# Turning q by the crossbar from chunk 2 on, in two halves, with the next chunk's loads planned behind the first half

## The chip, the cores and the metric

One core of a Trainium2 chip. The metric is device microseconds of one execution of the whole program on that core; medians of several runs are given. A program on one core has no second die to compare with, so a run counts as slow only if it lies over 1.5% above the fastest of its kernel; comparisons use the other runs.

Every ratio below is the mean time of one kernel's fast runs over that of the kernel before's fast runs of the same rounds on the same chip, so it is not quite the ratio of the quoted medians.

## The reference, cut to what matters

```python
kv  = einsum('bhsd,bhse->bhde', k, v)            # 8 batches, 8 heads, 576 rows, head size 64
out = einsum('bhsd,bhde->bhse', q, kv)
out = out / sqrt(mean(out*out, -1) + 1e-6) * g_norm
x   = out as [4608, 512]                          # rows of all batches, heads side by side
h   = x @ w_in                                    # [4608, 1024]
solu = h * softmax(h);  ln = layernorm(solu) * g_ln
return ln @ w_out                                 # [4608, 512], float32
```

## The kernel before

The rows are worked off in nine chunks of 512: chunk c below 8 is the first 512 rows of batch c, chunk 8 collects the last 64 rows of each batch. Per chunk TensorE makes k'v (`kv_mm`), o (`o_mm`, two halves of four heads), the sums of squares over heads (`s_mm`), eight projections (`h_mm`), the sums over d_ff and the eight halves of the output (`out_mm`). ScalarE does squares, logarithms and exponentials, VectorE (DVE) products and scaling, GpSimd (POOL) squares and sums in SBUF, and it also issues all loads that cast to bf16.

`o_mm` needs q with the head's columns on the partitions, so q has to be turned. Up to chunk 3 TensorE turns it (eight 128x128 transposes for each half of the heads, into the one PSUM bank `misc`, once into `h`, and a copy out); from chunk 4 on the DMA crossbar turns all of it from SBUF to SBUF, issued from the SP queue.

All instructions are ordered by a small list scheduler in the kernel (the planner). Each piece has an engine, an assumed length and a list of pieces that must be over first; pieces are put out in the order of their planned times. A piece that is listed as needed is an order in the plan. It is a semaphore wait on the chip only if the later instruction reads or overwrites what the earlier one wrote or read.

```python
class Plan:                                        # cut
    def order(self):
        ...
            if n[0] == "qT" and engine == "sp":    # a crossbar turn
                if queue > t + 1.0:                # loads still queued by the plan's reckoning
                    length, queue = 2.2 * length, queue + 2.0
            free[engine] = t + length
            done[n] = t + length + {"pe": 0.2, "sp": 2.5}.get(engine, 0.12)
            if load:
                queue = max(queue, t + length + 1.0) + load
                done[n] = queue + 1.3
...
    XBAR = tuple(range(4, NC))                     # chunks whose q the crossbar turns
...
    for b in range(B):                             # loads of k, v, q, issued from POOL
        behind = [] if b < 2 else [("h_mm", 0, 0)] if b == 2 else [("h_mm", b - 3, 2 if b == 3 else 0)]
        ...
    def q_turn(c):
        t = T["qT", c] = tile_of(("qT", c), [128, H, 2, 128], BF16)
        nc.sync.dma_start_transpose(
            t.rearrange("q h y p -> q (h y) p"), T["q", c].rearrange("p h j d -> p (h j d)")
        )
```

The softmax here doesn't subtract the row's maximum and nothing guards it: scores larger than these inputs give would overflow.

## Time and profile before

| | kernel before |
|---|---|
| median | 201.49 us (201.22 to 203.51, 4 runs) |
| span of the profiled run | 200.0 us, mean granted TensorE clock 0.996 |
| TensorE busy | 183.5 us (92%) |
| ScalarE / DVE / POOL busy | 141.1 / 125.0 / 128.7 us |
| first projection of chunk 1 | 48.01 us |
| first o of chunk 2 | 47.66 us |
| loads of chunks 3, 4, 5 leave POOL (k) | 30.70, 36.90, 64.02 us |

TensorE's share of the whole span says little; the prediction below shows the lines stretch by stretch.

### The profile page before, as it was taken

The page shows a single profiled execution, that of the slowest core. Times are in us where ns is not written, and L with a number is a line of the kernel's source. Part 1 is how long each engine was busy: PE and PEld are TensorE (multiplying, and loading weights), DVE is VectorE, ACT ScalarE, POOL GpSimd, SP SyncE. Part 2 cuts the span into 40 slices and gives each one's busy share as a digit, 9 for nine tenths or more (in the row PEclk, how much of TensorE's full clock was granted, in tenths as well). Part 3 has the DMA queues.
Part 4 walks back from the last instruction along what each step waited for, and adds up shares of the span by engine and source line. Part 5 has one row for each costly group of instructions (what it writes and reads, how often), then busy time and mean ns, then how long its engine had stood idle before and what let it go on. Part 6 is the DMA issues. An engine that isn't in the chain of part 4 may idle for free.

```text
span 200.0 us, 4091 instructions
## 1 busy us (share of the span) xinstructions
PE 183.5 (92%) x1614; PEld 83.3 (42%) x1614; DVE 125.0 (62%) x236; ACT 141.1 (71%) x244; POOL 128.7 (64%) x137
## 2 busy tenths in 40 slices
PE   7988986879699989999999899999999999999990
PEld 2342444345354435444444343544445454444430
DVE  3346669358785759768566856867594757665350
ACT  2028867986998799878889496979779386556421
POOL 7953679700699996957797487387484828846200
PEclk9999999999999999999999999999999999999998
DMA  4999999999994999999999982226021111211206
GB/s 51 178 198 286 326 200 201 202 203 239 248 200 67 151 200 167 196 196 223 186 166 197 179 210 69 107 71 157 17 91 52 52 56 52 108 52 52 107 11 198
DMA packets 39986, 29.62 MB, mean 148 GB/s; under 512 B 11800, under 2 KB 34336, under 8 KB 39968
## 3 DMA queue, kind: packets, MB, share of 16 engines
q0 software_dynamic: 24208, 17.30, 56.9%
q1 hardware_dynamic: 15472, 11.54, 19.8%
q10 hardware_dynamic: 288, 0.52, 0.9%
q8 instruction: 12, 0.20, 0.4%
q14 instruction: 6, 0.05, 0.1%
HBM read 32.51 MB, written 9.44 MB: 210 GB/s over the span
## 4 chain that ended last, share of the span: by engine, by line
PE 59%; DMA 20%; ACT 8%; POOL 6%; DVE 3%; issue 2%; POOLq 0%
PE out_ps L577 24%; PE h_ps L456 22%; DMA q_sb<-in_q_dram 11%; DMA w_out_f<-in_moe_w_out_dram 9%; PE misc_ps L520 4%; PE o_ps L337 3%; PE s_ps L358 3%; ACT rst_sb L366 2%; ACT e_sb L464 2%; PE o_ps L577 2%; ACT lss_sb L362 2%; POOL q_sb L230 1%; POOL v_sb L223 1%; DVE x_sb L379 1%; POOL k_sb L223 1%
## 5 line engine op out<-in xcount | busy, mean ns | idle before, releaser
L456 PE MATMUL h_ps<-x_sb,w_in_sb 128*128 128x512 bf16 x276 | 70.3, 379 | 2.2 <-DVE x_sb L379 1.2
L577 PE MATMUL out_ps<-w_out_sb,u_sb 128*128 128x512 bf16 x272 | 68.8, 379 | 0.8 <-DVE ob_sb L587 0.6
L482 POOL TENSOR_TENSOR usq_sb<-u_sb 128x512 bf16<-128x512 bf16 x51 | 52.7, 1042 | 22.0 <-DVE u_sb L471 21.7
L488 POOL TENSOR_TENSOR es_sb<-e_sb 128x512 bf16<-128x512 f32 x36 | 45.7, 1271 | 28.6 <-ACT e_sb L464 28.4
L471 DVE TENSOR_TENSOR u_sb<-h_ps,e_sb 128x512 bf16<-128x512 f32 x69 | 47.1, 687 | 25.6 <-ACT e_sb L464 25.1
L464 ACT ACTIVATE e_sb<-h_ps,zero_t 128x512 f32<-128x512 f32 x69 | 47.2, 685 | 15.5 <-PE h_ps L456 12.9
L456 PEld LDWEIGHTS <-w_in_sb 128*128 128x128 bf16 x288 | 27.1, 98 | 35.9 <-issue 5.7
L577 PEld LDWEIGHTS <-u_sb 128*128 128x128 bf16 x288 | 27.0, 98 | 34.0 <-issue 3.8
L587 DVE TENSOR_SCALAR ob_sb<-out_ps,rstd 128x512 f32<-128x512 f32 x33 | 24.4, 745 | 10.4 <-ACT rstd L556 5.4
L379 DVE SCALAR_TENSOR_TENSOR x_sb<-o_ps,g_rep,rst_sb 128x512 bf16<-128x512 f32 x32 | 23.9, 748 | 7.0 <-ACT rst_sb L366 6.7
L352 ACT ACTIVATE osq_sb<-o_ps,zero_t 128x512 bf16<-128x512 f32 x31 | 19.9, 683 | 9.4 <-PE o_ps L337 9.4
L366 ACT ACTIVATE rst_sb<-lss_sb,zero_t 128x512 f32<-128x512 f32 x32 | 23.3, 728 | 0.6
L362 ACT ACTIVATE lss_sb<-s_ps,eps_t 128x512 f32<-128x512 f32 x32 | 22.0, 688 | 0.6 <-PE s_ps L358 0.3
L480 ACT ACTIVATE usq_sb<-u_sb,zero_t 128x512 bf16<-128x512 bf16 x21 | 15.1, 720 | 4.9 <-DVE u_sb L471 4.9
L300 ACT CAST kvd<-misc_ps 64x128 bf16<-64x128 f32 (+1 forms) x24 | 7.5, 313 | 11.8 <-DVE kvd L298 11.3
L358 PE MATMUL s_ps<-osq_sb,head_mean 128*128 128x512 bf16 x34 | 12.9, 381 | 0.7 <-ACT lss_sb L362 0.4
L198 PE MATMUL s_ps<-zeros 128*128 128x512 bf16 x28 | 10.3, 498 | 1.4 <-DVE zeros L159 1.2
L230 POOL DMA_DIRECT2D q_sb<-in_q_dram x10 | 8.5, 854 | 4.2 <-DMA k_sb<-in_k_dram 1.6
L223 POOL DMA_DIRECT2D k_sb<-in_k_dram x10 | 7.8, 782 | 3.4 <-DMA w_in_sb<-in_moe_w_in_dram 1.8
L298 DVE CAST kvd<-misc_ps 64x256 bf16<-64x256 f32 (+1 forms) x16 | 6.1, 380 | 5.1 <-ACT kvd L300 3.1
L529 DVE STREAM_TRANSPOSE sumT_sb<-misc_ps 128x512 f32<-128x512 f32 x8 | 5.7, 711 | 5.7 <-PE misc_ps L520 5.7
L285 PEld LDWEIGHTS <-k_sb 96*64 96x64 bf16 x384 | 7.0, 112 | 4.1 <-issue 4.0
(81 smaller groups left out, 133.7 us busy)
## 6 DMA issues: line engine op xcount, KB each, us to landing
out_dram<-ob_sb SPq DMA_DIRECT2D x34, 256.0 KB, 2.5
k_sb<-in_k_dram POOLq DMA_DIRECT2D x6, 576.0 KB, 12.0
v_sb<-in_v_dram POOLq DMA_DIRECT2D x6, 576.0 KB, 12.1
q_sb<-in_q_dram POOLq DMA_DIRECT2D x6, 512.0 KB, 14.1
w_out_f<-in_moe_w_out_dram POOLq DMA_DIRECT2D x1, 2048.0 KB, 18.5
k_sb<-in_k_dram POOLq DMA_DIRECT2D x4, 288.0 KB, 12.6
v_sb<-in_v_dram POOLq DMA_DIRECT2D x4, 288.0 KB, 12.9
q_sb<-in_q_dram POOLq DMA_DIRECT2D x4, 256.0 KB, 13.1
```

The costliest lines, as they stand in the source:

```text
L352: nc.scalar.activation(out=t[:, :], in_=T[("o", *i)].rearrange("p a b c -> p (a b c)"), func=AF.Square, bias=zero_t[:, :])
L358: nc.tensor.matmul(t[:, :], head_mean[:, :], T["osq", i][:, :], start=True, stop=True)
L362: nc.scalar.activation(out=t[:, :], in_=T["s", i][:, :], func=AF.Ln, bias=eps_t[:, :])
L366: nc.scalar.activation(out=t.rearrange("p a b c -> p (a b c)"), in_=T["lss", i][:, :], func=AF.Exp, scale=-0.5, bias=zero_t[:, :])
L379: nc.vector.scalar_tensor_tensor(out=T["x", c][:, 2 * hf:2 * hf + 2, z], in0=T["o", c, hf, z][:, :, :, :], scalar=g_rep[:, :], in1=T["rst" ...
L456: nc.tensor.matmul(t[:, :], w_in_sb[:, dt, f * 128:(f + 1) * 128], T["x", c][:, dt].rearrange("p a b c -> p (a b c)"), start=(dt == 0), st ...
L464: nc.scalar.activation(out=T["e", c, f // 2][:, f % 2, :], in_=T["h", c, f][:, :], func=AF.Exp, bias=zero_t[:, :])
L471: nc.vector.tensor_tensor(out=T["u", c][:, f, :], in0=T["h", c, f][:, :], in1=T["e", c, f // 2][:, f % 2, :], op=MUL)
L482: nc.gpsimd.tensor_tensor(out=dst, in0=src, in1=src, op=MUL)
L488: nc.gpsimd.tensor_tensor(out=T["es", c][:, n, :], in0=e[:, 0, :], in1=e[:, 1, :], op=ADD)
L577: nc.tensor.matmul(T["acc", c, m][:, :], T["u", c][:, f, m * 128:(m + 1) * 128], w_out_sb[:, f, :], start=(f == 0), stop=(f == NF - 1),)
L587: nc.vector.tensor_scalar_mul(out=t[:, :], in0=T["acc", c, m][:, :], scalar1=T["rstd", c][:, m:m + 1])
```

## The change

Its intent: take the last turns off TensorE and the copies off DVE (chunks 2 and 3), let o of the first four heads start when half of the turn has landed, and keep the next chunk's loads out of the turn's way by planning them behind its first half.

```diff
-                    length, queue = 2.2 * length, queue + 2.0
+                    length, queue = 2.2 * length, queue + length
...
-    XBAR = tuple(range(4, NC))
+    XBAR = tuple(range(2, NC))
...
-        behind = ... [("h_mm", b - 3, 2 if b == 3 else 0)]
+        behind = ... [("qT", b - 1, 0)] + ([("h_mm", b - 3, 0)] if b > 3 else [])
...
-    def q_turn(c):
-        t = T["qT", c] = tile_of(("qT", c), [128, H, 2, 128], BF16)
+    def q_turn(c, hf):
+        if hf == 0:
+            T["qT", c] = tile_of(("qT", c), [128, H, 2, 128], BF16)
+        hs = slice(4 * hf, 4 * hf + 4)
         nc.sync.dma_start_transpose(
-            t.rearrange(...), T["q", c].rearrange("p h j d -> p (h j d)")
+            T["qT", c][:, hs].rearrange(...), T["q", c][:, hs].rearrange("p h j d -> p (h j d)")
         )
...
-            plan.add(("qT", c), "sp", 4.0, ...)
+            for hf in range(2):
+                plan.add(("qT", c, hf), "sp", 2.0, ...)
...
-                     [("qT", c) if c in XBAR else ("qT", c, hf), *kvs],      # what o_mm needs
+                     [("qT", c, hf), *kvs],
```

## The prediction

> **What bounds the kernel now.** I read the table of busy time by stretch first, because a share over the whole span mixes stages. Columns: stretch and its length; then for each engine busy us and instructions; last the granted clock, the DMA share and GB/s.
>
> ```profile
> core 0: us, PE busy (x) PEld busy (x) DVE busy (x) ACT busy (x) POOL busy (x), PEclk, DMA share, GB/s
> ...
> 40.00:48.00 8.00, 6.85 (x106) 3.91 (x106) 5.71 (x14) 5.58 (x11) 0.41 (x1) 1.00 1.32 220
> 48.00:56.00 8.00, 6.37 (x88) 3.27 (x85) 5.90 (x11) 7.29 (x13) 3.90 (x4) 1.00 1.28 237
> 56.00:64.00 8.00, 7.97 (x50) 3.68 (x48) 5.23 (x9) 7.38 (x13) 8.00 (x8) 1.00 0.82 118
> 64.00:72.00 8.00, 7.47 (x99) 3.52 (x97) 4.75 (x8) 6.33 (x13) 7.98 (x10) 1.00 1.14 167
> 72.00:80.00 8.00, 7.42 (x93) 3.60 (x90) 6.89 (x15) 7.87 (x17) 6.39 (x7) 1.00 1.10 181
> 112.00:120.00 8.00, 7.00 (x40) 2.96 (x38) 5.71 (x10) 5.71 (x10) 5.37 (x6) 1.00 0.84 193
> ```
>
> The reader is to see two regimes. From about 55 us on TensorE is close to full, and in every 8 us stretch from 80 to 192 us except the one at 112 it shows 8.00 of 8. There the end moves only with TensorE work taken away or with its few gaps (0.03 + 0.53 + 0.58 us between 56 and 80, 1.0 at 112). Before 56 us it has gaps: 1.15 and 1.63 us in the two stretches at 40 and 48, and 1.79 and 1.23 in those at 24 and 32 (not printed here). So the turns of q are worth their full TensorE time only where TensorE is full; earlier they lie partly in gaps.
>
> Then the timeline about the turns of chunks 2 and 3 that the change removes (start, duration, engine, line, operation, output <- inputs, count; in brackets the idle time before it and its releaser):
>
> ```profile
> 44.95 0.61 PE L308 MATMUL misc_ps<-ident,q_sb 128*128 128x128 bf16 x8
> ...
> 47.12 0.61 PE L308 MATMUL misc_ps<-ident,q_sb 128*128 128x128 bf16 x8
> ...
> 47.66 0.41 PE L337 MATMUL o_ps<-qT_sb,kvd 64*64 64x256 bf16 x8
> ...
> 48.12 1.26 ACT L352 ACTIVATE osq_sb<-o_ps,zero_t 128x512 bf16<-128x512 f32 x2 [1.53 <-PE o_ps L337]
> ...
> 54.02 1.27 ACT L464 ACTIVATE e_sb<-h_ps,zero_t 128x512 f32<-128x512 f32 x2
> ...
> 54.72 0.62 PE L308 MATMUL misc_ps<-ident,q_sb 128*128 128x128 bf16 x8 [1.63 <-DMA q_sb<-in_q_dram]
> ...
> 55.62 1.04 PE L456 MATMUL h_ps<-x_sb,w_in_sb 128*128 128x512 bf16 x4
> ```
>
> At 54.72 TensorE waited 1.63 us for chunk 3's q. That is not all the turn's fault: the next projection (55.62) needs an h bank, and those two banks are freed only after the two exponentials of 54.02 to 55.29 on ScalarE. ScalarE is busy 7.29 and 7.38 us of 8 here, so it is the pace-setter, and it had lost 1.53 us just before, waiting for chunk 2's o (48.12).
>
> Third, the turns and loads that exist already:
>
> ```profile
> L322 SPq DMA_TRANSPOSE qT_sb<-q_sb x4: 1631/1928/2036, 62.8 to 114.0; - x4
> ...
> DMA to landing us min/median/max: 4.3/4.4/6.8
> ```
>
> The minimum of 4.3 and the maximum of 6.8 us are a whole q (16 blocks of 128x128) on an otherwise quiet DMA and beside loads: the slow one, issued at 62.79, met chunk 5's loads from 64.02 on.
>
> **What the Trainium skill says.** "VectorE: DVE Perf Modes", section "The three transpose paths", gives 390 ns for a 128x128 bf16 turn on TensorE and 1309 ns by the crossbar. The trace has much less for both in a stream: eight turns in 0.61 us, sixteen crossbar blocks in 4.3 to 4.4 us. The measured ones decide, but the order is the same: the crossbar is slower and only pays because it frees engines. "Advanced Engine Details and Errata", section "X-Bar Transpose (TRN2)", expects 350-400 GB/s; 0.52 MB in 4.4 us is 119 GB/s with start-up, and while turns ran alone the DMA table showed some 210 to 220, so the trace does not agree. "DMA: Bandwidth & Descriptors", section "Issuing engines are not separate DMA queues", says that DMAs of all issuers share the 16 engines and interleave: the 6.8 against 4.3 us agrees. That is why the change plans loads behind the turn.
>
> **The change part by part.**
>
> Removed. Chunks 2 and 3 each lose two TensorE turns (8 matmuls, 0.61 us as shown, 0.45 us in the chain where pipelining overlaps them with the next work) and two DVE copies of 0.68 us (693 ns at most in the tile view). TensorE: 4 x 0.45 = 1.8 us, at most 4 x 0.61 = 2.4. DVE: 4 x 0.68 = 2.7 us, off the path, as DVE is busy 5.2 to 5.9 of 8 there. Of the TensorE time, the two turns of chunk 2 (44.95 and 47.12) lie where it waits anyway for x of chunk 1 (the first projection of chunk 1 starts at 48.01): worth 0. The turn at 54.72 is half hidden by ScalarE. The turn at 57.57 is in a full stretch: worth 0.45. Together 0.45 to 0.9.
>
> Added. Two more whole turns in halves, four crossbar issues, about 1 us of the SP queue each (estimate: half of 1.93), which is free there. A turn alone takes some 3.1 us of all DMA engines (the hardware queue's 31.2% share of the 10 us from 60 to 70). Cutting a turn in two should let the first half land about 1 us before the whole one would (estimate from the 1.9 us issue), so o of heads 0 to 3 can start earlier.
>
> Moved. The loads of chunk 3 are ordered after the first half-turn of chunk 2, no longer after the third projection of chunk 0. This is order on the POOL queue only, not a semaphore: POOL was idle from 40.4 to 50.8 us, so I expect them to go out as soon as chunk 0's last sums leave POOL, at about 34.5 instead of 30.70. Chunk 2's q then has the DMA more to itself and lands before 43.2 us (28.75 + 14.4 at present); I estimate 36 to 41. Add 4.4 to 6.8: its turn lands at 41 to 47.5, against a present DVE copy that ends at 46.5. So o of chunk 2 can start about 1 us earlier and fill part of the 1.53 us ScalarE gap: worth 1.1 us in a stretch that ScalarE paces. Chunk 4's loads move most: now at 36.90, they come behind chunk 3's first half-turn, at about 60 to 64. They must share POOL with the squares and sums of chunk 1, where POOL shows 8.00 of 8 busy; three issues of 0.8 to 0.9 cost 2.5 us of it.
>
> Sum: 0.7 (turns) + 1.1 (ScalarE starts chunk 2 earlier) + 0.4 (part of the gap at 48 to 56 that was the wait for q) - 0.6 (POOL and late loads, next part, weighted) = 1.6 us. 201.25 - 1.6 = 199.6 us.
>
> **The rivals.**
>
> *Late loads turn into TensorE waits.* The loads now form a cycle: load, turn, next load. From k's issue to q's landing takes 14.1 us (64.02 to 65.60 + 12.5), plus 4.4 for the turn: 18.5 us, while a chunk takes about 17.3 us of TensorE (sums at 104.48, 121.60, 138.78). If the plan thinks loads land sooner than they do, TensorE reaches the k-v product or o of chunks 4 and 5 before the data. At present those are at 68.0 and 77.8 for chunk 4; with loads at 60 to 64, v lands at 71 to 75 and the turn at 78 to 82. The planner knows of the delay and can put other projections first, and o of chunk 4 is needed only for h of chunk 4, far later. Against it too: the slack is regained later, as o of chunk 6 starts at 114.7 and its turn would land at about 111. Should it happen, 1 to 4 us are lost: 200.5 to 203.5.
>
> *POOL becomes the bound.* The one gap of TensorE after 80 us (1.0 at 113.66) came from such a thing: exponentials waited 2.25 us for POOL, which had been issuing loads at 99.8 to 102.8. One more chunk's issues in a busy stretch could make another gap of 1 us; moving the others could also remove this one. I put it at plus or minus 1.
>
> *The turns were hidden anyway.* Then only the 0.45 us remains and the time is 200.8.
>
> *More is freed than I count.* With no turns in the single misc bank of PSUM, and DMA relieved of chunk 4's loads until 55 us, all the gaps from 40 to 56 (2.8 us) could go, with the turns' 1.8: 196.7. Against it: ScalarE has 7.3 of 8 us of work there, which the change does not lessen.
>
> **Range and chances.** The best case gives 196.7, the bad one 203.5, the middle 199.6. I take 196.8 to 203.2 for 8 in 10. Faster by over 2% means under 197.2, which needs nearly every gap gone: 0.13. Slower by over 2% means over 205.3, worse than my stalls add up to: 0.08. Within 2%: 0.79.
>
> **What would show each step right or wrong.** No turns on TensorE after 40 us: 32 matmuls and 4 DVE copies fewer. The loads of chunk 3 near 34.5 us and of chunk 4 at 60 to 64. ScalarE's gap of 1.53 us before chunk 2's squares gone or under 0.5, and TensorE over 7 of 8 us in the stretch from 48 to 56. First half-turns that land in 3.5 to 6 us. The prediction is wrong if waits for k, v or turned q appear on TensorE at 66 to 96 us with more than 2 us in total, if the first projection of chunk 1 moves from 48 us by more than 2, or if the total falls below 197 because the gaps before 56 us had another cause than ScalarE.

## The result, and the profile after

The changed kernel takes 210.73 us (209.86 to 211.59, 4 runs) against 201.49: ratio 1.0436, interval 1.0355 to 1.0517. It is slower by over 2%, outside the range of the prediction. All its runs are of the fast state; the profiled one has a span of 208.8 us and a mean clock of 0.964.

The same table of stretches for the changed kernel, with the same columns:

```profile
40.00:48.00 8.00, 6.54 (x60) 2.98 (x54) 5.98 (x10) 5.99 (x12) 0.00 (x0) 1.00 1.28 230
48.00:56.00 8.00, 1.52 (x11) 0.58 (x11) 0.74 (x2) 0.96 (x3) 3.25 (x3) 0.65 1.33 177
56.00:64.00 8.00, 7.95 (x33) 2.99 (x33) 4.01 (x6) 5.51 (x10) 4.77 (x5) 0.71 0.40 78
64.00:72.00 8.00, 5.56 (x66) 2.59 (x66) 3.54 (x6) 5.69 (x10) 5.38 (x6) 0.93 0.01 2
72.00:80.00 8.00, 7.95 (x59) 2.95 (x59) 4.97 (x11) 6.70 (x13) 5.95 (x7) 0.86 1.01 142
```

From 48 to 56 us TensorE works 1.52 us where it had worked 6.37, ScalarE 0.96 instead of 7.29. The clock is granted at 0.65 to 0.93 in the stretches from 48 to 80 us; before, it was 1.00 in all of them. From 72 us on TensorE is nearly full again. From 48 to 72 us it works 15.0 us instead of 21.8, in part at the lower clock, so most of the loss is made there. Later marks agree, though pieces come in another order now: the sums over d_ff of chunk 2 (the squares' part) started at 83.89 us before and at 94.21 now, the last ones at 189.36 and 198.29, 8.9 us later.

The timeline of the changed kernel around it (POOL's issues of chunk 3's loads, the two half-turns of chunk 2, ScalarE, TensorE):

```profile
33.49 0.82 POOL L223 DMA_DIRECT2D k_sb<-in_k_dram  x1
34.30 0.77 POOL L223 DMA_DIRECT2D v_sb<-in_v_dram  x1
35.06 0.90 POOL L230 DMA_DIRECT2D q_sb<-in_q_dram  x1
...
42.48 6.88 SPq L324 DMA_TRANSPOSE qT_sb<-q_sb  x2
...
45.94 1.46 PE L459 MATMUL h_ps<-x_sb,w_in_sb 128*128 128x512 bf16 x6 [0.21 <-DVE x_sb L381]
...
54.48 0.64 PE L339 MATMUL o_ps<-qT_sb,kvd 64*64 64x256 bf16 x8 [7.08 <-DMA qT_sb<-q_sb]
...
55.16 1.27 ACT L354 ACTIVATE osq_sb<-o_ps,zero_t 128x512 bf16<-128x512 f32 x2 [7.04 <-PE o_ps L339]
```

The loads that were "planned behind the first half" of the turn left POOL at 33.49 us, nine microseconds ahead of that turn. Nothing on the chip made them wait for the turn: POOL issued them as soon as chunk 0's last sums were done (three sums from 29.82, 3.71 us) and had no other work before them. The turn was issued at 42.48, when chunk 2's q had just landed (27.85 + 14.2 = 42.05). TensorE then did two projections of chunk 1 and stood 7.08 us before the first o of chunk 2, and ScalarE stood as long.

How long the first half was under way until it landed, that is until its data had arrived, from the list of DMA issues, in a window that starts at its issue (count, then us from issue to landing):

```profile
qT_sb<-q_sb SPq DMA_TRANSPOSE x1, 12.0
```

And the DMA queues from 40 to 45 us (packets, MB, share). Queue q0 carries POOL's loads, q1 the stores and turns from SP:

```profile
q0 software_dynamic: 1387, 1.02, 132.4%
q1 hardware_dynamic: 1, 0.00, 0.1%
```

In these 5 us the loads moved 1387 packets. Queue q1 moved one, although a store had been issued at 41.45 and the turn at 42.48. The half-turn landed at 54.5 us, together with the last of chunk 3's loads (q: 35.06 + 19.6 = 54.7).

The lower clock fits the Trainium skill in kind: "TensorE: Matmul & The Clock Gate", section "Part 1: The HAM clock gate", says that the array falls to half clock after an idle window of about 3.4 us and comes back after a busy one. The lengths here are others: TensorE idled from 47.40 us, the clock was 1.00 until 50.2 and 0.50 from 50.4 on; work resumed at 54.48, and the clock was still 0.50 from 60.0 to 60.5. It fell once more at 70.8 us, after a wait of only 2.39 us.

### The profile page after: what moved, and what is told of

Same layout as the page of the kernel before. It is cut to its first block, busy times and chain, and to the rows that moved or that the text cites. A ratio compares the mean times of both kernels' runs of the same rounds, so it can differ in the third digit from the quotient of the medians.

```text
span 208.8 us, 4013 instructions
## 1 busy us (share of the span) xinstructions
PE 184.0 (88%) x1557; PEld 81.9 (39%) x1582; DVE 123.0 (59%) x232; ACT 142.3 (68%) x244; POOL 129.0 (62%) x137
## 4 chain that ended last, share of the span: by engine, by line
PE 63%; DMA 20%; DVE 4%; ACT 4%; POOL 4%; issue 2%; POOLq 0%; SPq 0%; ACTq 0%
PE h_ps L459 24%; PE out_ps L580 23%; DMA w_out_f<-in_moe_w_out_dram 8%; DMA qT_sb<-q_sb 7%; DMA v_sb<-in_v_dram 5%; PE misc_ps L523 4%; PE s_ps L360 3%; PE o_ps L339 3%; DVE w_out_sb L571 3%; PE misc_ps L285 2%; PE o_ps L580 2%; POOL k_sb L223 1%; PE out_ps L565 1%; ACT e_sb L467 1%; ACT osq_sb L354 1%
## 5 line engine op out<-in xcount | busy, mean ns | idle before, releaser
L459 PE MATMUL h_ps<-x_sb,w_in_sb 128*128 128x512 bf16 x265 | 72.7, 396 | 2.1 <-DVE x_sb L381 1.4
L580 PE MATMUL out_ps<-w_out_sb,u_sb 128*128 128x512 bf16 x260 | 67.0, 379 | 4.1 <-DVE u_sb L474 2.4
L459 PEld LDWEIGHTS <-w_in_sb 128*128 128x128 bf16 x288 | 28.0, 101 | 37.9 <-issue 9.7
L483 ACT ACTIVATE usq_sb<-u_sb,zero_t 128x512 bf16<-128x512 bf16 x21 | 15.1, 719 | 5.8 <-DVE u_sb L474 5.6
L339 PE MATMUL o_ps<-qT_sb,kvd 64*64 64x32 bf16 (+1 forms) x240 | 8.5, 265 | 7.7 <-DMA qT_sb<-q_sb 7.5
L360 PE MATMUL s_ps<-osq_sb,head_mean 128*128 128x512 bf16 x34 | 13.5, 397 | 0.3 <-ACT osq_sb L354 0.2
L198 PE MATMUL s_ps<-zeros 128*128 128x512 bf16 x27 | 9.7, 484 | 1.6 <-DVE zeros L159 1.2
L339 PEld LDWEIGHTS <-kvd 64*64 64x64 bf16 x256 | 4.6, 116 | 14.9 <-issue 14.0
L285 PE MATMUL misc_ps<-v_sb,k_sb 96*64 96x64 bf16 x384 | 8.0, 197 | 1.7 <-DMA v_sb<-in_v_dram 1.3
## 6 DMA issues: line engine op xcount, KB each, us to landing
w_out_f<-in_moe_w_out_dram POOLq DMA_DIRECT2D x1, 2048.0 KB, 17.3
```

The source lines that it names most:

```text
L360: nc.tensor.matmul(t[:, :], head_mean[:, :], T["osq", i][:, :], start=True, stop=True)
L459: nc.tensor.matmul(t[:, :], w_in_sb[:, dt, f * 128:(f + 1) * 128], T["x", c][:, dt].rearrange("p a b c -> p (a b c)"), start=(dt == 0), st ...
L580: nc.tensor.matmul(T["acc", c, m][:, :], T["u", c][:, f, m * 128:(m + 1) * 128], w_out_sb[:, f, :], start=(f == 0), stop=(f == NF - 1),)
```

## The experiments

Theory Q: chunk 2's turn queues in the DMA behind chunk 3's loads, and TensorE stands behind the turn. Rival L: the loads of chunks 4 to 7, moved behind turns, come too late. Rival S: turning in halves is dear. Beside these stood the question what the lower clock costs.

### Which part of the change: chunk 2's turn back on TensorE

```diff
-    XBAR = tuple(range(2, NC))
+    XBAR = tuple(range(3, NC))
```

> The changed kernel, but chunk 2's q is turned on TensorE again; chunk 3 stays on the crossbar in halves and the loads stay planned as in the change. Theory Q (chunk 2's turn queues in the DMA behind chunk 3's loads, which POOL issued 9 us before it; TensorE waits 7.1 us and then runs at a lower granted clock): the wait of 7 us before the first o of chunk 2 is gone, the mean clock is back over 0.99, 198.5 to 202 us. Rival L (the loads of chunks 4 to 7, now planned behind turns, come late): most of the loss stays, 206 to 210 us. Rival S (halved turns are dear in themselves): 204 to 208.

Measured: 203.15 us (202.87 to 203.78), ratio 1.0058 (1.0015 to 1.0101). Chunk 2's turn alone thus makes up nearly all of the loss: 1.0436 falls to 1.0058. The clock was 0.986 instead of the expected 0.99, and the time 1.15 us above the upper end of what theory Q expected. The profile shows waits for v (2.7 us in all, the longest 2.1), rival L in small; that they make up the rest is likely, but not shown.

### Which part of the change: chunks 2 and 3 back on TensorE

```diff
-    XBAR = tuple(range(2, NC))
+    XBAR = tuple(range(4, NC))
```

> The changed kernel with chunks 2 and 3 both on TensorE: what is left of the change is the halved turns from chunk 4 on and the loads planned behind turns. Theory Q: near the kernel before, 199.5 to 203 us, no wait of TensorE for a turn over 1 us. Rival L: 206 us or more, with waits of TensorE for k, v or q of chunks 4 to 7. Rival S: 203 to 207.

Measured: 201.74 us (201.41 to 204.62), ratio 0.9978 (0.9929 to 1.0028). Halved turns and moved loads, without the new turns, cost nothing that can be measured. Rivals L and S fall as main causes. One wait for a turn was 1.1 us, just over what was expected.

### What the lower clock costs

```diff
     def o_mm(c, hf, tag):
+        if (c, hf) == (2, 0):
+            for _ in range(30):
+                nc.tensor.matmul(<bank of o>, zeros[:, 0:128], zeros[:, :], start=True, stop=True)
```

> The changed kernel, with 30 matmuls on zeros (about 6.5 us at full clock) in front of the first o of chunk 2, into the bank that o then overwrites: TensorE works through the wait instead of idling. The turn still lands at about 54.5 us. If the lower clock after the wait (0.50 and 0.68 from 54 to 62 us) comes from the idle stretch, the clock stays near 1.0 there and the time falls by 3 to 5 us, to 205.5 to 207.5. If the clock falls for another reason, the time stays at 210 to 211.5.

Measured: 210.62 us (209.68 to 211.81), ratio 1.0443. The expectation failed. The first fence is the changed kernel from 56 us, in the table of stretches, the second the same stretches with the wait filled:

```profile
56.00:60.00 4.00, 4.00 (x11) 1.41 (x10) 0.86 (x2) 2.58 (x5) 1.16 (x2) 0.50 0.80 155
...
64.00:68.00 4.00, 3.73 (x60) 1.83 (x59) 2.15 (x4) 3.71 (x7) 2.85 (x3) 1.00 0.00 0
```

```profile
56.00:60.00 4.00, 3.47 (x16) 1.41 (x15) 2.05 (x3) 4.00 (x8) 1.95 (x2) 1.00 0.96 179
...
64.00:68.00 4.00, 2.12 (x29) 0.93 (x24) 2.37 (x5) 3.69 (x8) 1.73 (x3) 1.00 0.01 4
```

The filler did keep the clock: 1.00 from 56 to 60 instead of 0.50 (it fell only later, to 0.57 from 68 to 72), and TensorE got more done there. But ScalarE became full (4.00 of 4), and from 64 to 68 us TensorE idled 1.9 us instead of 0.3. At the sums of chunk 1 the filled kernel was 1.5 us ahead (73.07 against 74.59), at the last sums 1.0 (197.25 against 198.29), and in the medians 0.1. The clock drop is a consequence of the idling in the wait. The expected 3 to 5 us are out. A gain of a microsecond or two is not: the two profiled runs take 161.9 and 163.7 us from chunk 1's first projection (46.01 and 45.14) to the end. That little comes of it because ScalarE sets the pace in that stretch fits these lines, but was not tested.

### Making the planned order real

POOL reads a corner of the turned half before it issues chunk 3's loads, so that the semaphore wait is on the chip.

```diff
     def load_kv(name, src, b, hs):
+        if (name, b) == ("k", 3):
+            probe = big.tile([128, 128], BF16, name="probe")
+            nc.gpsimd.tensor_tensor(out=probe[:, :], in0=T["qT", 2][:, 0, 0, :], in1=T["qT", 2][:, 0, 0, :], op=MUL)
```

> The changed kernel, but POOL reads a corner of chunk 2's first turned half before it issues chunk 3's loads, so that they really go out behind the landing and not only in the plan. Theory Q: the first half lands within 5 us of its issue instead of 12.0, TensorE waits under 2 us for it, the clock stays over 0.98; chunk 3's loads leave at 45 to 48 us instead of 33.5; 199.5 to 204 us. If turns are slow there for another reason (the stores of chunk 0, or halving): the landing stays over 8 us and the time at 208 or more.

Measured: 203.98 us (203.44 to 206.56), ratio 1.0086 (1.0035 to 1.0136). The profile fell in the slow one of its runs, so the kernel was run again:

> The same kernel as in the run where chunk 3's loads wait for the first turned half, whose profile fell in a slow execution (206.56 us, against 203.4 to 204.2 in its three other runs). Expected: about 203.5 to 204.5 us; the first half lands 4.5 to 5.5 us after its issue; TensorE has no wait over 1 us for the turn, and what remains over the kernel before are waits for chunk 3's and later v, 3 to 6 us in all. If the waits for v were the slow execution's own, they are under 2 us here.

Measured: 204.65 us (203.52 and 205.78), ratio 1.0034, with an interval too wide (0.9854 to 1.0214; the kernel before had 203.73 on that chip). The readings agree with the first profile. The landing of the first half, in the same list of issues as above, and the waits of TensorE (us in total, times, longest) of the second run:

```profile
qT_sb<-q_sb SPq DMA_TRANSPOSE x1, 5.0
```

```profile
PE misc_ps L288 <- DMA v_sb<-in_v_dram: 3.7, 3, 2.6
...
PE o_ps L342 <- DMA qT_sb<-q_sb: 0.5, 1, 0.5
```

With the loads really behind it, the half landed in 5.0 us instead of 12.0, and the wait of 7.08 us was gone (0.5 in all). The price: chunk 3's loads leave at 49.0 us instead of 33.5, and k'v of chunk 3 waits 2.6 us for v. So the turn's delay came from those loads, and holding them back swaps a large wait for a smaller one. The stores of chunk 0 went out before the turn here too (at 41.43 us in the first of these runs), so by themselves they are not the cause.

### How much queue gives how much delay

Theory Q has two forms. Q1: a turn gets the DMA engines only when the loads queued before it have drained. Q2: a turn among loads takes a fixed multiple of its time. In the first run only q of chunk 3 is held back; its k and v go out as in the change.

```diff
     def load_q(b, hs):
+        if b == 3:
+            probe = big.tile([128, 128], BF16, name="probe")
+            nc.gpsimd.tensor_tensor(out=probe[:, :], in0=T["qT", 2][:, 0, 0, :], in1=T["qT", 2][:, 0, 0, :], op=MUL)
```

> The changed kernel, where only chunk 3's q load is held until the first half of chunk 2's turn has landed; its k and v go out as in the change. Q1: the turn has some 0.5 MB of 1.7 less in front of it, at 200 GB/s 2.6 us: it lands 8.5 to 10 us after its issue (12.0 in the change, 5.0 with all three held), 206 to 209 us. Q2: 11 to 13 us and 210 us or more.

Measured: 206.35 us (206.12 to 207.93), ratio 1.0238 (1.0175 to 1.0301). The half landed in 7.9 us, under the expected 8.5 to 10, and TensorE waited 3.0 us for it:

```profile
qT_sb<-q_sb SPq DMA_TRANSPOSE x1, 7.9
```

The fixed multiple (Q2) is out.

The other side: a turn that has six loads before it. Here nobody reads what the added turn writes.

```diff
 # in the kernel before
+        if c == 2:
+            spare = big.tile([128, H, 2, 128], BF16, name="spare")
+            plan.add(("spare", c), "sp", 4.0, r - 0.1, <turn of all of T["q", 2] into spare>, [("q", c, 0)], uses=[("q", c)])
```

> The kernel before, with one whole crossbar turn of chunk 2's q more, into a tile that nobody reads, issued as soon as that q has landed (about 43.5 us). The loads of chunks 3 and 4 are then both queued (issued from 30.7 to 40.4). Theory Q, in its sharp form Q1 (a turn gets its turn at the DMA engines only when the loads queued before it have drained): it lands at about 60 to 64 us, 16 to 20 us after its issue. Q2 (a turn among loads takes a fixed multiple, as the 12.0 us of the changed kernel): 11 to 13 us. The time moves little either way as nobody waits for it, 201 to 204 us; it shows what the crossbar's traffic costs without the wait.

Measured: 206.51 us (206.13 to 208.23), ratio 1.0238 (1.0168 to 1.0309). The spare turn landed 16.2 us after its issue at 42.32. That is in the range of Q1 in length, but at 58.5 us, before the expected 60, and chunk 4's q landed only at 66.4. The sharp form of theory Q is therefore wrong too: a turn doesn't wait until everything before it has drained. It comes in the later, the more is queued.

| run | loads issued before the turn and not yet landed | landing of the turn |
|---|---|---|
| planned order made real | none | 5.0 us (half) |
| q of chunk 3 held | k, v of chunk 3 | 7.9 us (half) |
| the changed kernel | k, v, q of chunk 3 | 12.0 us (half) |
| turns with unmoved loads (next) | all of chunks 3 and 4 | 15.6 us (whole) |
| the unused turn | all of chunks 3 and 4 | 16.2 us (whole) |

The packets say more of how. In the changed kernel, and in four of the runs around it (q of chunk 3 held, the unused turn, and the next two), q1 stood nearly still until the load then moving, chunk 3's k, had landed (at 44.7 to 45.4 us; in the change at 45.09). After that, while loads filled their queue, the two queues moved packets nearly one for one (in the unused turn 1346 and 1343 from 51 to 58 us). The changed kernel from 50 to 51 us, and below it the turn alone, from 47 to 48 us in the second run with the real order:

```profile
q0 software_dynamic: 237, 0.12, 87.4%
q1 hardware_dynamic: 237, 0.06, 46.4%
```

```profile
q1 hardware_dynamic: 812, 0.20, 90.9%
```

So a turn among these loads stood first and then ran at under a third of its packet rate. Why q1 stands still at first is not shown.

The time of the unused turn was a miss: I expected 201 to 204 us. It was 4.6 us slower than the kernel before in its rounds (201.90), and two views of it, the SP queue's timeline and TensorE's waits, show where 3.4 us of that came from:

```profile
66.53 6.24 SPq L322 DMA_TRANSPOSE qT_sb<-q_sb  x1
```

```profile
PE o_ps L337 <- DMA qT_sb<-q_sb: 3.4, 1, 3.4
```

The spare turn's traffic delayed chunk 4's q, so that chunk 4's own turn was issued at 66.53 us instead of 62.79. In the kernel before that turn went out 1.2 us ahead of chunk 5's loads and landed in 6.8 us. Now those loads were ahead of it, it landed in 15.1 us, and TensorE waited 3.4 us. The mechanism of the change hits another chunk, by the loss of a lead of 1.2 us.

### The turns without the moved loads, and a planner that knows

The kernel before with the crossbar from chunk 2 on, turns whole, loads unmoved:

```diff
 # in the kernel before
-    XBAR = tuple(range(4, NC))
+    XBAR = tuple(range(2, NC))
```

> The kernel before with crossbar turns from chunk 2 on, whole, and with the loads planned as before. Q1: chunk 2's turn waits for the loads of chunks 3 and 4, lands 15 to 20 us after its issue, TensorE waits over 10 us for it, 211 to 220 us: worse than the changed kernel, so that halving and moving loads did help. Q2: lands in 11 to 13 us, 207 to 211 us. Rival L (the moved loads are to blame): under 205 us.

Measured: 207.12 us (206.49 to 207.72), ratio 1.0250 (1.0199 to 1.0300). This fits neither form of theory Q: the turn landed late as in Q1 (15.6 us) and the time lies in the range of Q2, but TensorE waited only 1.14 us for the turn. With the loads of chunks 3 and 4 planned ahead, the planner reckoned with a full DMA (`queue > t + 1.0`) and put six projections of chunk 1 before o of chunk 2. In the change it believed the turn to be alone and put o right after two projections. So I told the planner of the changed kernel the truth, for chunk 2's o alone:

```diff
+        if c == 2:
+            for hf in range(2):
+                plan.add(("seen", hf), "delay%d" % hf, 7.5, r, lambda: None, [("qT", c, hf)])
...
-                     [("qT", c, hf), *kvs],
+                     [("qT", c, hf), *([("seen", hf)] if c == 2 else []), *kvs],
```

> The changed kernel, where the planner alone is told that o of chunk 2 can start only 7.5 us after it used to believe; queues, loads and turns keep their order, and TensorE gets all eight projections of chunk 1 ahead of the first o of chunk 2. Theory P (the late turn costs so much because TensorE, which takes its instructions in order, stands behind it): the turn still lands at 53 to 56 us, TensorE waits under 1.5 us for it, the clock stays over 0.98, 202 to 206 us. Rival T (chunk 2's attention being late is the cost, in whatever order TensorE works): 208 us or more.

Measured: 206.94 us (205.43 to 207.51), ratio 1.0193 (1.0138 to 1.0247), between the two expectations; the clock, 0.972 in the profile, was under the expected 0.98. TensorE waited for no turn any more, although the half took 11.5 us. But the idling came later, as these stretches show (same columns as above):

```profile
56.00:60.00 4.00, 4.00 (x69) 2.05 (x63) 2.10 (x4) 3.15 (x6) 4.00 (x5) 1.00 0.87 154
60.00:64.00 4.00, 1.54 (x22) 0.55 (x24) 1.50 (x2) 2.63 (x5) 4.00 (x6) 1.00 0.22 15
64.00:68.00 4.00, 2.31 (x26) 0.65 (x19) 1.98 (x6) 3.32 (x8) 0.49 (x1) 0.56 1.28 194
```

By 60 us the projections of chunk 1 were used up, and chunk 2's x was not there. Of the 4.4 points of loss, 2.4 (1.0436 to 1.0193) go away with the order of TensorE's instructions. The remaining 1.9 stay in this one other order; that the lateness of chunk 2's attention costs them in any order is argued, not shown, and the order of POOL and the other engines changed with it.

### Two attempts at a better kernel, and halving alone

Chunk 2's q loaded ahead of its k and v, with chunk 3's loads held as above:

```diff
-            plan.add(("q", b, g), ..., at + part + (0.02 if b < 2 else 0.1), ...
+            plan.add(("q", b, g), ..., at + part + (0.02 if b < 2 else -0.1 if b == 2 else 0.1), ...
```

> The changed kernel with chunk 2's q loaded ahead of its k and v, and chunk 3's loads held until the first half of that turn has landed. Theory Q: q lands at 34 to 37 us, the first half within 5 us of its issue, chunk 3's loads leave at 38 to 42 us (33.5 in the change, 48.0 with the wait alone), neither a wait of over 2 us for the turn nor one for k and v of chunk 3; clock over 0.98; 199.5 to 203 us. If the crossbar itself is what costs in this stretch: 205 or more.

Measured: 205.21 us (204.80 to 207.69), ratio 1.0181 (1.0109 to 1.0253): a miss. The turn was issued at 36.44 us as hoped, but chunk 2's own k and v were then ahead of it, it landed in 7.1 us, and chunk 3's loads left at 44.15. TensorE waited 4.3 us for v in all and 2.3 for turns. Its 205.21 us lie in the range that I had given to the crossbar being dear in itself; as the turn had loads ahead of it again, the run doesn't decide that. No run shows what chunk 2's turn is worth with neither the turn nor chunk 3's loads late.

Halving alone in the kernel before (`q_turn(c, hf)` as in the diff of the change, nothing else):

> The kernel before with its crossbar turns (chunks 4 to 8) in halves and nothing else. Halving in itself is harmless: 200.5 to 202.5 us, ratio 0.995 to 1.005, halves land in 3.1 to 4 us. If halving costs: over 203.

Measured: 202.29 us (202.11 to 204.36, 6 runs), ratio 1.0003 (0.9960 to 1.0047). Halving is free and gains nothing by itself; the halves landed in 3.2 us (median).

The last attempt keeps chunks 2 and 3 on TensorE and the halved turns, and moves only chunk 3's loads. In the profile after, chunk 1's first projection had started at 45.14 us instead of 48.01, since chunk 0's sums on POOL no longer had three load issues between them.

```diff
 # in the changed kernel
-    XBAR = tuple(range(2, NC))
+    XBAR = tuple(range(4, NC))
-        behind = ... [("qT", b - 1, 0)] + ([("h_mm", b - 3, 0)] if b > 3 else [])
+        behind = ... [("qT", 2, 0)] if b == 3 else [("h_mm", b - 3, 0)]
```

> The kernel before with halved turns and with chunk 3's loads alone moved behind chunk 2's turn (on TensorE); the loads of chunks 4 to 7 as before. Chunk 0's sums on POOL are then no longer held up by three load issues and the first projection of chunk 1 starts at 45 to 46 us instead of 48.0, while later loads are not late: 199 to 201.5 us, ratio 0.985 to 1.0. If the early start is given back to ScalarE: 201 to 202.5.

Measured: 200.60 us (200.11 to 201.72, 6 runs), ratio 0.9907 (0.9870 to 0.9945): faster than both kernels by the interval, if under 2%. Its first projection of chunk 1, in TensorE's timeline:

```profile
46.20 1.04 PE L459 MATMUL h_ps<-x_sb,w_in_sb 128*128 128x512 bf16 x4
```

That is 1.8 us earlier than before, and 1.9 us of the 202.47 (the median of the kernel before in these rounds) came out at the end. That the two numbers are alike is no proof that one is the other.

## Why the prediction was wrong, point by point

- **What bounds the kernel: right.** TensorE full late, ScalarE pacing the stretch from 48 to 64 us. The filled wait agrees: with TensorE's clock at 1.00 from 56 to 60 us ScalarE was full (4.00 of 4), and the time was the same within the noise.
- **What is removed: right in the counts.** No turn on TensorE after 40 us. What it was worth was never seen, as the loss covered it.
- **When chunk 3's loads leave: right.** Predicted about 34.5 us, as an order on POOL only; measured 33.49.
- **When chunk 2's q lands: off.** Predicted 36 to 41 us; measured 42.05, only 1.1 us earlier than before.
- **"Add 4.4 to 6.8": the step that failed.** I gave the turn its landing times from the kernel before. Those turns had been issued on a quiet DMA or 1.2 us ahead of the loads (62.79 against 64.02). This one was issued 9 us behind three loads (by my own numbers, loads at 34.5 and q at 36 to 41, it would have been 1.5 to 6.5 us) and took 12.0 us, as a half. I saw that the loads would run ahead of the turn and did not carry it into the turn's duration. The run with the real order (5.0 us) and the one with two loads (7.9 us) settle it. (The sum itself gives 40.4 to 47.8, not 41 to 47.5; that changes nothing. Likewise the three sums named under late loads lie 17.15 us apart, not 17.3.)
- **"Worth 1.1 us" for ScalarE's gap: the sign was wrong.** The gap of 1.53 us became 7.04. Another order on TensorE gave back 2.4 of 4.4 points; that the rest hangs on chunk 2's attention being late is likely.
- **The rival of late loads: there, but small.** Waits for v of 1.3 us in the profile after; halving and moving without new turns measured 0.9978. I had expected such waits to be the way in which the change could lose, and put the danger at chunks 4 and 5 when it was at chunk 2.
- **The rival of POOL:** no run shows a loss from it in the changed kernel. The opposite came: without the three load issues chunk 0's sums on POOL were done earlier, and the first projection of chunk 1 started at 45.14 us instead of 48.01. A move of over 2 us was one of my signs of being wrong; it is a gain that I had not counted, and the last attempt keeps it. Chunk 4's loads left at 72.25 us, not 60 to 64, as chunk 1 itself was late.
- **The range:** its upper end, 203.2, held stalls of up to 4 us. No stall of 7 us for the turn was in it, and "slower by over 2%" had 0.08.

## What to carry to other kernels

A dependency in a scheduler's plan orders instructions only within one queue. Between two queues it holds on the chip only if a semaphore makes it hold, so look whether the queue of the later piece has anything else to do before it. Take a transfer's duration from a case with the same traffic issued ahead of it. And before giving a transfer a place in the middle of a load stream, ask which engine's in-order stream will stand behind it.

## What the Trainium skill lacked or had wrong

- "DMA: Bandwidth & Descriptors", sections "Queues, rings and completion order" and "Issuing engines are not separate DMA queues": they say that each engine takes its queue rows in turn, packet by packet, and that issuers interleave. From 50 to 51 us the trace agrees, in that both queues moved 237 packets. It doesn't before 45 us: from 40 to 45 us q1 moved 1 packet beside 1387 of q0, with a store issued at 41.45 us and a turn at 42.48. Neither section tells that such a standstill comes first; why it does is not shown here.
- The second of these sections calls the issue time usually small beside the DMA itself. A half-turn's issue took 1.25 us in a quiet stretch and 4.56 us behind chunk 3's loads, in a landing of 12.0.
- "Advanced Engine Details and Errata", section "X-Bar Transpose (TRN2)": it has transposes as fast as other DMAs and 350-400 GB/s. A whole turn of 0.52 MB on a quiet DMA landed in 4.3 to 4.4 us, which is 119 GB/s with start-up. While only turns moved, from 57 to 58 us in the changed kernel, it was 0.26 MB in 1 us, 260 GB/s.
- "TensorE: Matmul & The Clock Gate", section "Part 1: The HAM clock gate": agreed with in kind, but not in its window of about 3.4 us: the clock fell within 3.0 us of idling (47.40 to 50.4 us) and once after a wait of 2.39 us, and it came back only after more than 6.0 us of work (54.48 to over 60.5 us).
